# Weight loads behind all stage-one transposes, one more chunk with denominators in token order, and layer-two work chunk by chunk, in a two-layer linear-attention and MLP kernel

## The chip, the cores and the metric

One core of one Trainium2 chip. The metric is device microseconds (us) of one execution; lower is better. A kernel is compared by several timed executions, beside executions of the kernel before on the same chip. The span that a profile shows is from the first to the last instruction; in the runs here the time is the span plus about 1.75 us.

## The reference, cut to what matters

Two layers run one after the other on one sequence of 2,048 tokens with 512 features, all bf16. `A` is linear attention with 32 heads of 16, `B` an MLP of hidden size 1,792.

```python
def _A_ref(x, wqkv, wo):
    qkv = (x @ wqkv) ...                       # q, k, v: heads of 16
    phi = lambda t: jnp.where(t > 0, t + 1, jnp.exp(t)) + 1e-6
    pq, pk = phi(q), phi(k)
    kv  = jnp.einsum("bhsd,bhse->bhde", pk, v)     # a sum over ALL tokens
    z   = jnp.einsum("bhsd->bhd", pk)              # likewise
    num = jnp.einsum("bhqd,bhde->bhqe", pq, kv)
    den = jnp.einsum("bhqd,bhd->bhq", pq, z)[..., None] + 1e-6
    return (num / den) ... @ wo

def _B_ref(x, w1, b1, w2, b2):
    h = gelu(layernorm(x) @ w1 + b1)
    return h @ w2 + b2

x = A_x
for _ in range(2):                             # written out in the original
    x = x + _A_ref(_layernorm(x), A_wqkv, A_wo)
    x = x + _B_ref(_layernorm(x), B_w1, B_b1, B_w2, B_b2)
```

Because `kv` and `z` sum over all tokens, the kernel has a first stage ("stage one") that normalizes, transposes and projects all 16 tiles of 128 tokens before the first output of layer one. Four tiles are a chunk.

## The kernel before

Every operation is recorded in a graph with an engine, a duration estimate and a priority. A list scheduler then fixes the order on each engine, together with the PSUM banks and buffers. `SHIFT` moves priorities by group or name; `WAY` picks one of several ways to do the same thing (for instance, a transpose by TensorE or by DMA). The order is then replayed, each engine waiting on semaphores.

```python
def transpose(y, ykey, yT, k, key, prio, tag):          # by DMA, issued from SyncE
    ...  e.dma_start_transpose(dst, yb[:, y.slot, :])   # L647: "t<-yb" in the profile
def transpose_pe(...):                                  # by TensorE (L660), then a copy out of PSUM
    ...  e.transpose(...);  e.activation(dst(), src(), ACT.Copy)      # L670, on ACT

def attn_k(L, c, k, yT, prio):                          # K projection (L711) and phi(K)
    ...  e.matmul(bank(b), lhsT=yTa(yT)[:, dt, k*P:(k+1)*P], rhs=wqkv[:, dt, D:2*D], ...)
    phi(b, ...)                                         # exp (L681), relu (L692), min, add (L698)

def late(name, key, dst, src, prio, kb, after):         # weight loads on POOL's queue
    dma("pool", lambda e: e.dma_start(dst, src), [key], prio=prio, name=name, kb=kb, after=after)
...
pq1, trs = [], []
for c in range(NC):                                     # stage one
    for k in range(4):
        y, ykey = norm(...)
        if eng(f"TA0_{st}") == "pe":  tr = transpose_pe(...)
        else:                         tr = transpose(...)
        ...
        pk = attn_k(0, c, k, yT, pr + 3)
        attn_g_held(0, st, k, y, ykey, pk, gb, pr + 6)
    attn_z(0, c, pks, pr + cf["P_Z0"])
    trs.append(tr)                                      # the last tile of each chunk only
    attn_q(0, c, yT, pq, ...)
for h in range(2):
    late(f"w1_{h}", ..., -86 + h, 896, trs)             # L581 in the profile: four loads of 896 KB
for h in range(2):
    late(f"w2_{h}", ..., -84 + h, 896, trs)
dma("sp", lambda e: e.dma_start_transpose(b1t[:], b1r[:]), ..., name="Tb1", after=trs[-1:])
G.op("act", lambda e: e.activation(b1c[:], b1t[:, 0:FT], ACT.Copy), ..., name="b1c")
```

`Tb1` is the "bias transpose": it turns the bias of the up-projection into one column per partition, for the GELU. `b1c` is its copy on ACT. ACT works in the order that the scheduler fixed, so whatever stands behind `b1c` waits for `Tb1`.

The denominators of a chunk have two forms. By default they are four matmuls with 512 columns, then Ln and Exp on ACT. With `"den0_2": "tok"` (layer, chunk) they are a product and a reduction on POOL and DVE in token order, and a DMA transpose for each tile.

Of the kernel before, what the change touches and what calls it, by code (L numbers as in the profile page):

```python
# [19 lines left out]
NC = S // 512  # L20
# [32 lines left out]
class Op:  # L53
    __slots__ = ("eng", "fn", "dur", "lat", "deps", "tiles", "prio", "name", "table", "sem", "nbytes",
                 "idx", "start", "end", "ready", "missing", "outs", "waits", "tok", "opens", "seq", "fast", "n", "grp")

    def __init__(self, eng, fn, dur, lat, prio, name, table=None, sem=None, nbytes=0, fast=False, n=1):
        self.eng, self.fn, self.dur, self.lat = eng, fn, dur, lat
        self.prio, self.name, self.table, self.sem, self.nbytes = prio, name, table, sem, nbytes
        self.fast, self.n = fast, n  # L60
        self.deps = {}
        self.tiles = []
        self.opens = []
        self.outs = []
        self.start = self.end = None
        self.ready = 0.0
        self.tok = None
# [43 lines left out]
class Scheduler:  # L111
# [13 lines left out]
    def run(self):  # L125
        g = self.g
        for o in g.ops:
            o.missing = len(o.deps)
        for o in g.ops:
            for d in o.deps:  # L130
                d.outs.append(o)
# [11 lines left out]
        while left:  # L143
# [36 lines left out]
            at, _, o = best  # L180
            e = o.eng
# [35 lines left out]
            for w in o.outs:  # L217
                w.missing -= 1
                w.ready = max(w.ready, o.end + self.latency(o, w))
                if w.missing == 0:  # L220
                    released[w.eng].append(w)
# [70 lines left out]
def assign_waits(graph, order, sems, dma_sems):  # L292
# [10 lines left out]
    while len(done) < total:  # L303
# [45 lines left out]
    N_HALF=1, N_K=3, N_Q=2, P_Z0=7.85, N_PB=1, N_PT=8, P_DEN=-8.22, P_A2=-25.68, P_W1=-3.82, P_W2=73.83,  # L349
    P_K=47.84, P_G=106.63, P_Q=169.99, STEP=5.46, A1_Q=25.3, A1_STEP=4.8, N_H=2, N_N=2, GAP=37.5,  # L350
    TABLE_PENALTY=17.25, WINDOW=104.97,
    SHIFT={
        "B00_0": -200.0, "B00_1": -230.4, "B00_2": -43.8, "B00_3": -75.1, "B01": 573.6, "B02": 68.1,
        "B03": 1079.8, "B10_0": 139.0, "B10_1": 57.7, "B10_2": 195.5, "B10_3": 32.2, "B11": 392.5,
        "B12": 42.9, "B13": -84.8, "D00": -507.8, "D01": -19.7, "D02": 60.8, "D03": 290.1, "D0_0_3": 4.5,
        "D10": -22.9, "D11": -10.1, "D12": -16.4, "D13": 645.3, "G00_0": -7.9, "G00_1": 0.3, "G00_2": -138.2,
        "G00_3": -20.1, "G01_0": 28.9, "G01_1": -111.0, "G01_2": -39.9, "G01_3": -92.7, "G02_1": 5.5,
        "G02_2": 506.5, "G02_3": 62.7, "G03_0": -7.0, "G03_1": -43.1, "G03_2": 69.5, "G03_3": 59.5,
        "G10": 26.6, "G11": 54.3, "G12": 223.3, "G13": 8.1, "G1_2_0": 12.9, "K00_0": -436.6, "K00_1": -27.0,
        "K00_2": -31.4, "K00_3": 1.1, "K01_0": 3.7, "K01_1": -0.5, "K01_2": -12.5, "K01_3": -49.4,  # L360
        "K02_0": -2.3, "K02_1": 260.6, "K02_2": 13.8, "K03_0": 325.9, "K03_1": 272.3, "K03_2": -18.8,
        "K03_3": -116.2, "K0_0": 1.8, "K10": 76.8, "K11": 10.2, "K12": 74.9, "K13": -130.7, "K1_12": -2.7,
        "M0_2": 114.0, "N00_0": -371.7, "N00_1": -416.2, "N00_2": -206.3, "N00_3": -0.2, "N01_0": -506.7,
        "N01_1": 4.0, "N01_2": -116.3, "N01_3": 38.6, "N02_0": 7.6, "N02_1": 213.7, "N02_2": 62.3,
        "N02_3": 130.0, "N03_0": 47.7, "N03_1": 274.9, "N03_2": 165.0, "N03_3": -5.7, "N10": 29.9,
        "N11": 399.0, "N12": -2.5, "N13": 125.5, "O00_0": 113.8, "O00_1": -55.4, "O00_2": -13.0,
        "O00_3": -80.3, "O01": -191.1, "O02": 6.3, "O03": 6.1, "O10_0": 26.6, "O10_1": 179.5, "O10_2": 39.8,
        "O10_3": 196.8, "O11": -847.0, "O12": 12.5, "O13": 13.6, "OD11": -0.6, "OD8": 17.6, "PTA0_1": 5.0,
        "Q00": 486.1, "Q01": 4.9, "Q02": 544.3, "Q03": 790.2, "Q10": 264.7, "Q11": 89.7, "Q12": 850.4,
        "Q13": 202.3, "RA1_1": -1.0, "RA1_3": -2.8, "RB0_11": 5.5, "RB1_10": -4.5, "RB1_2": -2.1,  # L370
        "TA1_1": 2.6, "TA1_10": -2.5, "TA1_11": 7.6, "TA1_14": -12.7, "TB0_12": -8.0, "TB0_14": 7.8,
        "TB0_9": 5.0, "TP1_3_0": 10.2, "Tb1": 57.1, "U00_0": -32.4, "U00_1": 55.7, "U01": -34.1, "U02": -18.3,
        "U03": 10.5, "U10_1": 70.5, "U11": 17.1, "U12": -5.9, "U13": 105.3, "V0": 17.1, "V1": 34.2,
        "W00": 448.9, "W01": 288.7, "W02": -13.4, "W03": 10.3, "W10": 7.5, "W10_0_10_0": 12.9,
        "W10_0_8_0": -1.0, "W10_2_7_0": 6.9, "W10_3_9_0": 6.4, "W11": -34.5, "W11_0_6_1": -4.4,
        "W11_2_11_0": 9.4, "W12": -25.5, "W13": 58.8, "W20_3_7": -15.8, "W21_0_0": -10.8, "W21_0_7": 4.5,
        "W21_12_0": -70.7, "W21_3_7": 1.0, "W21_5_0": -0.7, "W21_5_7": 2.4, "W21_7_0": 26.0, "WO0_12_0": 34.3,
        "WO0_13_0": -36.5, "WO0_3_0": -14.3, "WO1_12_0": -21.7, "WO1_6_0": -0.7, "Z00": -23.1, "Z01": 0.8,
        "Z03": -77.1, "Z11": -19.4, "Z12": -118.0, "Z13": 27.2, "aggrB0_10": -1.5, "aggrB1_11": 10.0,
        "aggrB1_12": 4.3, "b20_8": -0.4, "b21_8": -28.4, "cpm0_1": 4.9, "cpz1": -15.6, "expk1_1": 74.7,  # L380
        "expk1_15": 5.5, "expq0_1_3": -2.2, "expq0_3_1": 2.7, "expq1_1_2": 3.4, "expq1_1_3": -1.2,
        "gelu0_0_0_1": -3.5, "gelu0_0_4_1": -26.0, "gelu0_1_2_0": -12.0, "gelu0_2_0_0": -1.8,
        "gelu0_2_6_0": -3.0, "gelu1_0_11_0": 4.6, "gelu1_0_6_0": 82.2, "gelu1_0_7_0": 1.4,
        "gelu1_0_8_1": -58.6, "gelu1_0_9_0": -48.9, "gelu1_1_5_0": 2.1, "gelu1_2_13_0": -2.6,
        "gelu1_3_6_0": -3.7, "ln0_1_0": 1.5, "ln0_2_2": -1.2, "ln0_3_3": 42.5, "mink0_1": 8.8,
        "mink0_14": -49.7, "mink1_11": -33.7, "mink1_14": -7.0, "mink1_8": 17.3, "minq0_0_0": -47.6,
        "minq0_0_3": -0.5, "minq0_3_3": -5.3, "minq1_2_3": 2.6, "nmrA0_11": 0.3, "normA0_12": 7.2,
        "normA1_0": -16.0, "normA1_10": 23.2, "normB1_3": 15.7, "phik0_10": -12.4, "phik0_15": 6.8,
        "phik0_5": 7.7, "phik0_6": -11.7, "phik0_9": 14.9, "phik1_11": 9.9, "phik1_8": 0.5,
        "phiq1_2_0": -12.4, "phiq1_3_2": -5.4, "powA0_6": -3.5, "powA1_1": -0.2, "powB0_11": 16.2,  # L390
        "powB0_3": -4.8, "pr0_0_2": -6.6, "pr0_3_0": -9.1, "pr1_0_0": 2.4, "rec0_1_3": -2.2, "rec0_2_1": -4.3,
        "rec1_0_1": -1.3, "rec1_1_3": -1.5, "reluk0_0": -5.7, "reluk0_12": 30.2, "reluk0_13": -34.0,
        "reluk0_8": -0.3, "reluk1_11": 2.2, "statsA1_12": -24.9, "statsA1_2": 3.7, "statsA1_4": 2.7,
        "statsA1_6": 8.2, "statsB0_11": 1.8, "statsB0_2": -44.8, "statsB0_3": 2.5, "statsB1_11": 3.1,
        "statsB1_4": 6.6, "tcA0_5": 10.4, "tcA0_7": 15.9, "tcB1_1": -8.8, "vepsA0_12": -2.8, "vepsA0_4": 3.8,
        "vepsA1_14": -59.9, "vepsA1_4": -3.8, "vepsB0_13": -85.9, "vepsB0_4": -1.1, "vepsB0_6": 1.3,
        "vepsB1_5": 12.9, "vepsB1_9": -27.4, "warm": -0.5, "x1": 1.4,
# [4 lines left out]
        "TA0_6": "dma", "TA0_7": "pe", "TA0_8": "pe", "TA0_9": "dma", "TA1_0": "dma", "TA1_1": "pe",  # L402
        "TA1_10": "pe", "TA1_11": "pe", "TA1_12": "pe", "TA1_13": "pe", "TA1_14": "pe", "TA1_15": "dma",
        "TA1_2": "pe", "TA1_3": "pe", "TA1_4": "pe", "TA1_5": "pe", "TA1_6": "pe", "TA1_7": "pe",
        "TA1_8": "pe", "TA1_9": "pe", "TB0_0": "dma", "TB0_1": "pe", "TB0_10": "dma", "TB0_11": "dma",
        "TB0_12": "dma", "TB0_13": "dma", "TB0_14": "dma", "TB0_15": "dma", "TB0_2": "dma", "TB0_3": "dma",
        "TB0_4": "dma", "TB0_5": "dma", "TB0_6": "dma", "TB0_7": "pe", "TB0_8": "dma", "TB0_9": "dma",
        "TB1_0": "dma", "TB1_1": "pe", "TB1_10": "dma", "TB1_11": "dma", "TB1_12": "dma", "TB1_13": "dma",
        "TB1_14": "dma", "TB1_15": "dma", "TB1_2": "dma", "TB1_3": "dma", "TB1_4": "dma", "TB1_5": "dma",
        "TB1_6": "dma", "TB1_7": "dma", "TB1_8": "dma", "TB1_9": "dma", "b20_0": "pool", "b20_1": "dve",  # L410
        "b20_10": "dve", "b20_11": "dve", "b20_12": "dve", "b20_13": "pool", "b20_14": "pool",
        "b20_15": "dve", "b20_2": "dve", "b20_3": "pool", "b20_4": "dve", "b20_5": "dve", "b20_6": "pool",
        "b20_7": "pool", "b20_8": "pool", "b20_9": "pool", "b21_0": "pool", "b21_1": "pool", "b21_10": "pool",
        "b21_11": "dve", "b21_12": "dve", "b21_13": "dve", "b21_14": "dve", "b21_15": "pool", "b21_2": "dve",
        "b21_3": "pool", "b21_4": "dve", "b21_5": "dve", "b21_6": "pool", "b21_7": "dve", "b21_8": "dve",
        "b21_9": "dve", "cpg0_0": "dve", "cpg0_1": "dve", "cpg0_2": "dve", "cpg0_3": "act", "cpg1_0": "dve",
# [39 lines left out]
def build_kernel(nc, A_x, A_wqkv, A_wo, B_x, B_w1, B_b1, B_w2, B_b2, out, conf=None, report=False):  # L456
# [5 lines left out]
    with ExitStack() as es:  # L462
# [13 lines left out]
        b1r = SB("b1r", [16, P], BF16)  # L476
# [743 lines left out]
```

## Time and profile before

| | |
|---|---|
| time, median of 3 runs | 334.19 us (334.19 to 334.74) |
| the run whose profile was kept | 336.87 us, span 335.1 us, mean granted clock 0.995 |
| first up-projection of layer one | at 70.06 us |

To the views that the prediction shows further down I add only the page's strip of 40 equal slices of 8.4 us; each digit is tenths busy, and PEclk is the granted TensorE clock in tenths:

```profile
PE   7899699999999999999999999999999999999997
PEclk9999799999999999999999999999999999999999
DMA  7814920020124003200001110001152222101001
```

In the fifth slice (33.5 to 41.9 us), PE falls to 6, the clock to 7, and the DMA engines are at 9. Nothing like it follows.

### The profile page before, as it was taken

The numbers are of one execution on the slowest core, as the hardware profiler recorded it, in microseconds if no ns is written. First come the engines' busy times: TensorE is split into PE (matmuls) and PEld (weight loads), VectorE is DVE, ScalarE is ACT, GpSimd is POOL, SyncE is SP. The second block draws the span as 40 slices with busy tenths as digits, with TensorE's granted clock in tenths as the row PEclk, the third lists the DMA queues.
The fourth block names the chain that finished last, engine by engine and source line by source line (L and its number), as shares of the span: only waits on it lengthen the run. The fifth ranks groups of instructions, "written<-read, shape, count | busy, mean of one in ns | idle before, by whom it ended". The sixth has DMA issues, their size and how long they took to land.

```text
span 335.1 us, 4774 instructions
## 1 busy us (share of the span) xinstructions
PE 326.5 (97%) x1742; PEld 160.9 (48%) x1742; DVE 214.5 (64%) x455; ACT 217.5 (65%) x366; POOL 138.1 (41%) x227
## 2 busy tenths in 40 slices
PE   7899699999999999999999999999999999999997
PEld 3444244478444444444444444447744444444444
DVE  6889466892694887205375799899899697122012
ACT  2698479999998716999623466988936601730640
POOL 5688325763483537212124362578606042020000
PEclk9999799999999999999999999999999999999999
DMA  7814920020124003200001110001152222101001
GB/s 265 268 34 85 344 92 0 2 47 2 38 56 51 16 16 80 48 0 16 18 0 31 33 32 1 2 17 33 32 120 53 63 62 66 31 6 59 16 4 60
DMA packets 40116, 18.42 MB, mean 55 GB/s; under 512 B 33756, under 2 KB 39132, under 8 KB 40092
## 3 DMA queue, kind: packets, MB, share of 16 engines
q1 hardware_dynamic: 36524, 10.90, 15.0%
q0 software_dynamic: 1056, 4.72, 4.3%
q10 hardware_dynamic: 2512, 2.49, 2.2%
q8 instruction: 14, 0.23, 0.3%
q14 instruction: 10, 0.08, 0.1%
HBM read 8.00 MB, written 2.10 MB: 30 GB/s over the span
## 4 chain that ended last, share of the span: by engine, by line
PE 86%; ACT 8%; DMA 2%; DVE 1%; issue 1%; POOL 1%
PE ps L986 29%; PE ps L1024 28%; PE ps L711 6%; PE ps L954 6%; PE ps L838 4%; PE ps L742 4%; PE ps L806 3%; DMA t<-yb 2%; PE ps L729 2%; ACT eb L681 2%; PE ps L596 1%; ACT yb L632 1%; ACT rb L692 1%; ACT lr L932 1%; PE ps L930 1%; ACT lr L934 1%
## 5 line engine op out<-in xcount | busy, mean ns | idle before, releaser
L986 PE MATMUL ps<-t,w 128*128 128x512 bf16 (+1 forms) x560 | 99.5, 336 | 0.0
L1024 PE MATMUL ps<-w,gT 128*128 128x512 bf16 x434 | 98.4, 379 | 0.0
L992 ACT ACTIVATE gT<-ps,b1c 128x512 bf16<-128x512 f32 (+1 forms) x140 | 80.5, 603 | 23.6 <-PE ps L986 23.2
L986 PEld LDWEIGHTS ps<-t,w 128*128 128x128 bf16 x560 | 54.6, 98 | 42.8 <-ACT t L670 0.6
L1024 PEld LDWEIGHTS ps<-w,gT 128*128 128x128 bf16 x434 | 42.4, 98 | 50.8
L681 ACT ACTIVATE eb<-ps 128x512 bf16<-128x512 f32 x64 | 38.6, 611 | 15.6 <-PE ps L711 13.5
L632 ACT ACTIVATE yb<-xsb,nmr,rstd 128x512 bf16<-128x512 f32 x23 | 18.5, 808 | 41.3 <-POOL nmr L629 39.0
L692 ACT ACTIVATE rb<-ps 128x512 bf16<-128x512 f32 x54 | 32.9, 616 | 12.6 <-PE ps L711 11.5
L624 POOL TENSOR_TENSOR rstd<-veps,neghalf 128x1 f32<-128x1 f32 x64 | 38.2, 597 | 6.8 <-DVE veps L622 1.9
L711 PE MATMUL ps<-wqkv,t 128*128 128x512 bf16 x128 | 32.7, 394 | 3.0 <-DMA t<-yb 2.8
L612 DVE BATCH_NORM_STATS2 stats<-xsb 128x6 f32<-128x512 f32 x48 | 32.5, 681 | 0.4
L694 DVE TENSOR_SCALAR eb<-eb 128x512 bf16<-128x512 bf16 x54 | 16.9, 319 | 23.4 <-ACT eb L681 22.9
L954 PE MATMUL ps<-gtb,t 128*128 128x512 bf16 x128 | 31.2, 379 | 0.2 <-ACT gtb L819 0.2
L938 POOL TENSOR_TENSOR t<-t,lr 128x512 bf16<-128x512 bf16 x18 | 21.6, 1199 | 18.6 <-ACT lr L934 18.6
L617 POOL TENSOR_SCALAR veps<-mv 128x1 f32<-128x1 f32 x32 | 7.0, 219 | 50.5 <-DVE mv L614 48.7
L1034 DVE TENSOR_TENSOR outb<-ps,xsb 128x512 bf16<-128x512 f32 x15 | 10.2, 682 | 26.3 <-PE ps L1024 26.2
L622 POOL TENSOR_SCALAR veps<-mv 128x1 f32<-128x1 f32 x29 | 8.1, 278 | 41.8 <-DVE mv L614 41.2
L742 PE MATMUL ps<-t,wqkv 128*128 128x512 bf16 x96 | 23.5, 379 | 0.0
L1030 DVE TENSOR_TENSOR xsb<-ps,xsb 128x512 f32<-128x512 f32 x16 | 10.9, 681 | 18.0 <-PE ps L1024 17.9
L711 PEld LDWEIGHTS ps<-wqkv,t 128*128 128x128 bf16 x128 | 12.5, 100 | 19.2 <-issue 4.9
L637 DVE TENSOR_SCALAR yb<-xsb,mv,rstd 128x512 bf16<-128x512 f32 x25 | 17.6, 703 | 4.7 <-POOL rstd L624 4.4
L959 DVE TENSOR_TENSOR xsb<-ps,xsb 128x512 f32<-128x512 f32 x16 | 10.7, 683 | 15.1 <-PE ps L954 15.1
(90 smaller groups left out, 389.2 us busy)
## 6 DMA issues: line engine op xcount, KB each, us to landing
w<-in_B_w_dram POOLq DMA_DIRECT2D x4, 896.0 KB, 9.2
out_dram<-outb SPq DMA_DIRECT2D x15, 128.0 KB, 1.8
t<-in_A_x_dram ACTq DMA_DIRECT2D x3, 512.0 KB, 8.2
t<-yb SPq DMA_TRANSPOSE x53, 2.4
wqkv<-in_A_wqkv_dram SPq DMA_DIRECT2D x1, 512.0 KB, 5.5
wqkv<-in_A_wqkv_dram ACTq DMA_DIRECT2D x1, 512.0 KB, 7.3
wqkv<-in_A_wqkv_dram POOLq DMA_DIRECT2D x1, 512.0 KB, 6.2
wo<-in_A_wo_dram POOLq DMA_DIRECT2D x1, 512.0 KB, 5.8
```

Source lines behind the costliest of these rows:

```text
L612: G.op("dve", lambda e: e.bn_stats(stats[:, s.slot, :], src()), 620, reads=src_keys, writes=[k + "s"], tiles=[s, *src_tiles], prio=prio, n ...
L624: G.op("pool", lambda e: e.tensor_tensor(rstd[:, s.slot:s.slot + 1], veps[:, s.slot:s.slot + 1], neghalf[:], op=ALU.pow), 570, reads=[k + ...
L632: G.op("act", lambda e: e.activation(yb[:, y.slot, :], src(), ACT.Identity, bias=nmr[:, s.slot:s.slot + 1], scale=rstd[:, s.slot:s.slot + 1]),
L681: G.op("act", lambda e: e.activation(eb[:, et.slot, :], bank(bt), ACT.Exp), 478, reads=[src_key], writes=[f"e{tag}"], tiles=[bt, et], prio ...
L692: G.op("act", lambda e: e.activation(rb[:, rt.slot, :], bank(bt), ACT.Relu), 478, reads=[src_key], writes=[f"r{tag}"], tiles=[bt, rt], pri ...
L711: ins = e.matmul(bank(b), lhsT=yTa(yT)[:, dt, k * P:(k + 1) * P], rhs=wqkv[:, dt, D:2 * D], start=(dt == 0), stop=(dt == DT - 1))
L742: ins = e.matmul(bank(b), lhsT=wqkv[:, dt, kt * P:(kt + 1) * P], rhs=yTa(yT)[:, dt, :], start=(dt == 0), stop=(dt == DT - 1))
L938: lambda e, kt=kt, r=r: e.tensor_tensor(yTa(pq)[:, kt, :], yTa(pq)[:, kt, :], lr[:, r.slot, :], op=ALU.mult),
L954: ins = e.matmul(bank(wb), lhsT=yTa(pq)[:, kt, k * P:(k + 1) * P], rhs=gtb[:, kt, :], start=(kt == 0), stop=(kt == DT - 1))
L986: ins = e.matmul(bank(b, n), lhsT=w1[:, dt, ft * P:(ft + 1) * P], rhs=yTa(yT)[:, dt, k0 * P:k1 * P], start=(dt == 0), stop=(dt == DT - 1))
L992: G.op("act", lambda e, ft=ft, b=b, k0=k0, k1=k1, n=n: e.activation(gT[:, g.slot, ft * 512 + k0 * P:ft * 512 + k1 * P], bank(b, n), ACT.Ge ...
L1024: ins = e.matmul(bank(b), lhsT=gT[:, g.slot, ft * 512 + k * P:ft * 512 + (k + 1) * P], rhs=w2[:, ft, :], start=(ft == 0), stop=(ft == FT - 1))
```

## The change

The intent: (1) the MLP weights shall not be loaded while stage one still needs DMA transposes, so all 16 tiles' transposes, not only the last of each chunk, go into the list that the loads wait for, and the bias transpose waits for that list too; (2) the third chunk of layer one takes its denominators in token order, which takes four matmuls from PE, adds one, and takes Ln/Exp pairs from ACT; (3) layer two's normalizations, phi(K) and G (the sum over tokens of normalized rows times phi(K)) are tied chunk to chunk by predecessors that only bind the scheduler (`soft`), so that its buffers are used in chunk order. All priorities and choices were then tuned again for the new graph.

```diff
@@ scheduler: predecessors that order, but are no data
-            o.missing = len(o.deps)
+            o.soft = [d for d in o.soft if d not in o.deps]
+            o.missing = len(o.deps) + len(o.soft)
-            for d in o.deps:
+            for d in [*o.deps, *o.soft]:
                 d.outs.append(o)
...
-                w.ready = max(w.ready, o.end + self.latency(o, w))
+                if o not in w.soft:
+                    w.ready = max(w.ready, o.end + self.latency(o, w))
@@ CONF (cut: some 200 lines of SHIFT and WAY are new throughout)
-    N_HALF=1, N_K=3, N_Q=2, P_Z0=7.85, ...  A1_Q=25.3, ...  GAP=37.5,
-    TABLE_PENALTY=17.25, WINDOW=104.97,
+    N_HALF=1, N_K=4, N_Q=2, P_Z0=0.37, ...  A1_Q=81.1, ...  GAP=0,
+    TABLE_PENALTY=25.46, WINDOW=126.58,
-        "TA0_6": "dma", "TA0_7": "pe", "TA0_8": "pe", "TA0_9": "dma", ...
+        "TA0_6": "dma", "TA0_7": "dma", "TA0_8": "dma", "TA0_9": "dma", ...
+        "den0_2": "tok", ...                      (and many phi forms)
@@ stage one
+                trs.append(tr)
                 pk = attn_k(0, c, k, yT, pr + 3)
...
             attn_z(0, c, pks, pr + cf["P_Z0"])
-            trs.append(tr)
...
-        dma("sp", ... b1t ... name="Tb1", after=trs[-1:], transpose=True)
+        dma("sp", ... b1t ... name="Tb1", after=trs, transpose=True)
@@ before the scheduler runs
+        named = {o.name: o for o in G.ops}
+        for c in range(1, NC):
+            for k in range(4):
+                for n in ("normA1_{}", "phik1_{}"):
+                    named[n.format(4 * c + k)].soft += [named[n.format(4 * (c - 1) + i)] for i in range(4)]
+                named[f"G1_{c}_{k}"].soft.append(named[f"G1_{c - 1}_{k}"])
```

Lines of the changed kernel stand six to thirteen lower in the file than before: L711 becomes L717, L986 becomes L992.

## The prediction

> **What bounds the kernel now.** I read the engine shares first, then who TensorE (PE) waited for, then the chain of work that ended last in order of time, then the stretch around the one long wait.
>
> The head of the page:
>
> ```profile
> span 335.1 us, 4774 instructions
> PE 326.5 (97%) x1742; PEld 160.9 (48%) x1742; DVE 214.5 (64%) x455; ACT 217.5 (65%) x366; POOL 138.1 (41%) x227
> ```
>
> PE is busy 97% of the span, but a busy PE need not be at its peak, so I counted its work instead. The chain gives the pitch of each kind of matmul where PE runs unhindered:
>
> ```profile
> 70.22 12.23 PE ps L986 x112
> 96.92 10.36 PE ps L986 x48
> 227.72 0.22 PE ps L660 x4
> 206.76 0.38 PE ps L787 x16
> ```
>
> That is 0.109 us for 256 columns, 0.216 us for 512, 0.055 us for a transpose or another 128-column matmul, 0.024 us for the one-column sums. Times the counts: 1,315 of 512 columns 283.8 us, 252 of 256 columns 27.5 us, 76 of 128 columns 4.1 us, 88 one-column sums 2.1 us, and the 11 warm-up matmuls 4.9 us: 322.4 us. The span is 335.1 us, so 12.7 us are lost. Cutting the chain at its own times (elapsed less work of the matmuls in that stretch) places them:
>
> - before PE's first matmul: 1.5 us
> - 1.51 to 30.52 (start of stage one): 29.0 elapsed, 26.8 work, 2.2 lost
> - 30.52 to 43.46: 12.9 elapsed, 8.15 work, **4.8 lost**
> - 43.46 to 57.31: 0.1 lost
> - 57.31 to 70.22 (to the first up-projection): 12.9 elapsed, 11.9 work, 1.0 lost
> - 70.22 to 332.66 (everything else): 262.4 elapsed, 261.8 work, 0.6 lost
> - after PE's last matmul: 2.4 us
>
> So four fifths of the run have nothing left except matmuls to remove, and one stretch holds over a third of the loss. The waits of PE, longest first, say what ended its idle time:
>
> ```profile
> PE ps L711 <- DMA t<-yb: 2.8, 1, 2.8
> PE ps L596 <- DVE onesm L560: 1.5, 1, 1.5
> PE ps L660 <- DVE yb L637: 1.0, 1, 1.0
> ```
>
> L711 is a K projection; it waited for a DMA transpose of normalized rows. The chain there:
>
> ```profile
> 29.61 0.22 DVE t L698
> 29.83 1.00 issue
> 30.82 0.16 DVE t L698
> 30.99 7.04 DMA t<-yb
> 38.03 0.14 issue
> 38.16 3.57 PE ps L711 x8
> 41.73 1.73 PE ps L742 x8
> ```
>
> That transpose was issued at 30.99 and landed 7.04 us later. Eight K matmuls after it took 3.57 us, 0.45 each, twice the usual pitch. The transposes of that stage and, in the timeline, the MLP weight loads on POOL's queue:
>
> ```profile
> DMA to landing us min/median/max: 2.4/2.5/7.0
> 30.57 1.53 POOL L581 DMA_DIRECT2D w<-in_B_w_dram  x2
> 33.20 1.90 POOL L581 DMA_DIRECT2D w<-in_B_w_dram  x2
> ```
>
> The median is 2.5 us; only the transpose issued 0.4 us after the first weight load took 7.0. The view of three windows (columns: window and its length, busy of PE, weight load, DVE, ACT, POOL, then granted clock, DMA share, GB/s) completes it:
>
> ```profile
> 26.00:31.00 5.00, 5.00 (x39) 2.53 (x38) 4.57 (x11) 5.00 (x12) 3.88 (x6) 1.00 0.35 71
> 31.00:38.10 7.10, 4.40 (x23) 1.76 (x19) 5.84 (x12) 4.00 (x8) 5.02 (x6) 1.00 0.98 262
> 38.10:43.50 5.40, 5.33 (x17) 2.09 (x18) 1.39 (x5) 2.81 (x6) 0.20 (x1) 0.68 0.98 344
> ```
>
> DMA goes from 35% to 98% busy; the granted clock falls to 0.68 after the gap. The 4.8 us are thus 2.8 us of idle PE, and about 2 us of slow matmuls after it.
>
> **What the Trainium skill says.** (1) "Perfetto Trace Analysis", section "Identifying the Most-Contended Engine": matmul busy share is no good measure of headroom. The trace agrees: 97% busy, 12.7 us lost. (2) "DMA: Bandwidth & Descriptors", section "Issuing engines are not separate DMA queues": DMAs from scalar, sync or gpsimd run on the same 16 engines and interleave. The trace agrees: a SyncE transpose beside POOL's loads took 7.0 instead of 2.5 us. (3) "TensorE: Matmul & The Clock Gate", section "HAM oscillation": idle gaps of over about 3.4 us put PE back to half clock. Here a 2.8 us gap was followed by 0.45 us matmuls, so half clock followed a gap shorter than that figure. (4) "ScalarE: Activation LUTs", section "What ACT_TABLE_LOAD costs": 1283 ns for a load plus a drain, 2.66 us together. The trace has 1,283 ns for each of 16 loads.
>
> **The change, part by part.** A list scheduler places every instruction by priorities, and the diff replaces nearly all of these; so I compared the built orders.
>
> *Weights behind all transposes.* Before, the four weight loads waited for the last tile of each chunk; a transpose issued after those fell beneath the loads. Now they wait for all of stage one's transposes (10 by DMA, 8 before). This removes the 7.0 us landing: at 2.5 us it would end at 33.5, before the K projection ahead of it ended (34.37 + 0.86 = 35.2). Saved: up to 4.8, I take 4.4 us, leaving 0.4 for ordinary unevenness. The weights come later by perhaps 3 us: their median landing was 9.2 us, so from about 34 on to 46, against a first use near 65. Hidden.
>
> *PE work.* Transposes on PE go from 44 to 40 (-4 x 0.055 = -0.22); chunk two's denominators in token order remove four denominator matmuls (-4 x 0.216 = -0.86) and add one that spreads the sums (+0.22). Q is the same count in another form. Sum -0.86 us; PE is the bound, so I count it whole.
>
> *ACT before the first GELU.* Six fewer Relu (6 x 0.62 = 3.7), two fewer Ln and Exp pairs (2 x 1.38 = 2.8), two fewer transpose copies (1.2), one fewer late normalization (0.8); three more early ones (3 x 0.84 = 2.5), one copy (0.6). Net about -5.4 us of 53 busy in the first 70. That matters: ACT stands on the chain from 53 to 68, and its work falls by more than the stall that is removed, so it should not take the stall's place.
>
> *DVE in the same stretch.* To the eighth residual add: six more max forms reading PSUM (6 x 0.69 = 4.1), three fewer normalizations (-1.5), one reduction and reciprocal (0.67 + 0.33 + 0.28), one diagonal (about 1.0), other changes near zero: +5 us on 51.7. But POOL's 2-input adds there go from 7 to 2, and DVE adds that ran beside those took up to 1.73 us instead of 0.42, so part comes back.
>
> *Later.* K may hold four PSUM banks instead of three, table loads fall from 16 to 14, and layer two's normalizations, its phi(K) and G go chunk by chunk. 0.6 us is all that these could win after 70; they can only lose.
>
> Sum: 335.1 - 4.4 - 0.86 = 329.8 us span, that is 5.3 less; from 334.19: 328.9. I add 0.5 us for new small stalls, since an order with all priorities changed is unlikely to hit the 0.6 us of the old one again: **329.4 us**.
>
> **Rivals.** *DVE becomes the bound of stage one.* For: 56 us of work in some 65. Against: the POOL adds that slowed it go. It would give back 2 to 4 us: 331.5 to 333.5. *The bias transpose stalls ACT.* It now waits for all ten transposes, and ACT's order has the bias copy before nine of its 30 exponentials; ACT could stand still for the 2.3 us that this transpose took. For: ACT runs in order. Against: four K banks absorb some. Cost 0 to 2 us: up to 331.5. *A table load or the chunk order opens a gap in the middle.* The new order puts three switch pairs among chunk two's GELUs, each pair 2.6 us of ACT beside about 3 us of PE work. Against: the old order had such pairs at 0.6 us in all. 1 to 3 us: 330.5 to 332.5. *The start gets better too.* The 2.2 and 1.0 us losses could halve with less ACT work: 327.8. *The stall is only moved:* ten transposes at 1.26 us of issue each might land late without any load beside them: 332 to 334.
>
> **Range and chances.** All removable loss gone (4.8 + 2.2 + 1.0 + 0.6, and 0.86 of work) is 9.5 us: 324.7, a floor. Over 2% faster is below 327.5, which needs 6.7 us, more than the stall and the removed work together (5.7): 0.13. Slower by 2% needs a loss larger than any above: 0.02. Range 327.2 to 332.2.
>
> **What would show it.** Right: no landing of a stage-one transpose much over 2.5 us, weight loads issued after the last of them, no PE wait of over 1 us on a DMA, a clock near 1.00 in every window after the warm-up, first up-projection near 65 instead of 70.2. PE's count lower by four transposes and three 512-column matmuls. Wrong: a new PE wait on DVE or ACT between 20 and 65, ACT idle before the bias copy, or the time from the first up-projection to the last matmul over 263 us, which was 262.4.

## The result, and the profile after

The changed kernel takes 334.14 us (median of 4 runs, 333.71 to 334.76), against 334.19 us (334.11 to 334.74, 4 runs) for the kernel before. The ratio is 0.9996, with a 95% interval of 0.9976 to 1.0017: the same. A ratio here is the mean time of one kernel's runs over the mean of the other's runs of the same rounds, so not quite the ratio of the medians. Executions over 1.5% slower than the fastest of the same kernel are left out of the means. The prediction was 329.4 us with a range of 327.2 to 332.2; the measured time lies outside it.

The head of the page after:

```profile
span 332.2 us, 4772 instructions
PE 324.7 (98%) x1735; PEld 159.6 (48%) x1735; DVE 219.1 (66%) x461; ACT 208.7 (63%) x348; POOL 146.8 (44%) x238
```

The span fell by 2.9 us against the profile before, while the time did not fall. The two profiles are thus not of runs that stand for their kernels in the same way; the first experiment settles that. PE's waits after, longest first (in all us, how often, longest):

```profile
PE ps L602 <- DVE onesm L566: 1.5, 1, 1.5
PE ps L793 <- DVE pkb L704: 0.8, 1, 0.8
PE ps L717 <- DMA t<-yb: 0.7, 2, 0.4
PE ps L666 <- DVE yb L643: 0.6, 1, 0.6
PE ps L992 <- ACT t L676: 0.4, 1, 0.4
```

The 2.8 us wait for a transpose is gone. No single wait of size has come in its place, but several small ones have. The first new one is L793, the one-column sums over phi(K). In the chain in order of time (start, us, what), what releases it is the bias transpose:

```profile
31.50 2.39 DMA t<-yb
...
33.91 4.61 DMA b1t<-b1r
...
38.55 0.21 ACT b1c L1085
38.76 0.48 ACT eb L687
39.24 0.50 ACT rb L698
...
39.83 0.44 DVE pkb L704
...
40.31 0.55 PE ps L793 x16
```

The last stage-one transpose lands at 33.89. That releases both the bias transpose, at 33.91, and the weight loads, of which the trace shows the first at 34.2 and the last at 36.7. The bias transpose takes 4.61 us to land; in the profile before it took 2.3. The next line is ACT's wait, from ACT's view of 8 to 70 us:

```profile
ACT b1c L1085 <- DMA b1t<-b1r: 1.4, 1, 1.4
```

ACT stands still for 1.4 us, then exp, relu and the addition follow one after another, and PE loses 0.8 us. The landings of stage one's ten transposes, in one line:

```profile
DMA to landing us min/median/max: 2.4/2.5/4.2
```

None takes 7.0 us any more. But one takes 4.2 and two more over 3 us, with no weight load beside them. So the prediction's last rival ("the stall is only moved") came true in part; what these landings share is shown after the last run of the changed kernel.

To place the loss I took each kernel's trace, counted its matmuls at the unhindered pitch as the prediction does, and cut at the first up-projection of layer one and of layer two. All in us:

| profile of | span | clock | work | lost in stage one | in layer one | in layer two and tail |
|---|---|---|---|---|---|---|
| before, the one kept | 335.1 | 0.995 | 322.4 | 9.48 | 0.54 | 2.69 |
| before, again | 332.8 | 1.000 | 322.4 | 7.17 | 0.56 | 2.68 |
| changed | 332.2 | 1.000 | 321.5 | 6.13 | 1.84 | 2.71 |
| changed, again | 333.0 | 1.000 | 321.5 | 6.97 | 1.86 | 2.70 |

So the changed kernel saves its 0.86 us of work, saves only 0.2 to 1.0 us in stage one against a run of before at full clock, and loses 1.3 us more in layer one.

### The profile page after: what moved, and what is told of

Read it like the earlier page. It is cut to its first block, busy times and chain, and to the rows that moved or that the text cites. A ratio compares the mean times of both kernels' runs of the same rounds, so it can differ in the third digit from the quotient of the medians.

```text
span 332.2 us, 4772 instructions
## 1 busy us (share of the span) xinstructions
PE 324.7 (98%) x1735; PEld 159.6 (48%) x1735; DVE 219.1 (66%) x461; ACT 208.7 (63%) x348; POOL 146.8 (44%) x238
## 4 chain that ended last, share of the span: by engine, by line
PE 78%; DVE 9%; DMA 5%; POOL 4%; ACT 3%; issue 1%; DVEq 0%; POOLq 0%
PE ps L1030 27%; PE ps L992 26%; PE ps L960 8%; PE ps L717 4%; PE ps L748 3%; PE ps L844 3%; DMA t<-yb 3%; PE ps L735 2%; PE ps L812 2%; POOL rstd L630 2%; DMA b1t<-b1r 1%; DVE gtb L828 1%; DVE yb L643 1%; DVE stats L618 1%; DMA t<-in_A_x_dram 1%; PE ps L936 1%
## 5 line engine op out<-in xcount | busy, mean ns | idle before, releaser
L992 PE MATMUL ps<-t,w 128*128 128x512 bf16 (+1 forms) x560 | 99.3, 337 | 0.4 <-ACT t L676 0.4
L1030 PE MATMUL ps<-w,gT 128*128 128x512 bf16 x434 | 97.3, 379 | 0.0
L992 PEld LDWEIGHTS ps<-t,w 128*128 128x128 bf16 x560 | 54.5, 98 | 44.0 <-ACT t L676 1.5
L717 PE MATMUL ps<-wqkv,t 128*128 128x512 bf16 x128 | 30.9, 380 | 1.2 <-DMA t<-yb 0.7
L944 POOL TENSOR_TENSOR t<-t,lr 128x512 bf16<-128x512 bf16 x10 | 11.6, 1163 | 36.4 <-ACT lr L940 36.4
L623 POOL TENSOR_SCALAR veps<-mv 128x1 f32<-128x1 f32 x32 | 8.8, 274 | 41.2 <-DVE mv L620 39.5
L698 ACT ACTIVATE rb<-ps 128x512 bf16<-128x512 f32 x41 | 24.8, 609 | 3.3 <-PE ps L748 2.3
L1036 DVE TENSOR_TENSOR xsb<-ps,xsb 128x512 f32<-128x512 f32 x16 | 10.7, 675 | 23.7 <-PE ps L1030 23.7
L977 POOL TENSOR_TENSOR xsb<-xsb,b2b 128x512 f32<-128x512 f32 x19 | 22.5, 1192 | 3.1 <-DVE yb L643 2.0
L700 DVE TENSOR_SCALAR eb<-eb 128x512 bf16<-128x512 bf16 x41 | 15.1, 378 | 11.2 <-ACT eb L687 11.1
L628 POOL TENSOR_SCALAR veps<-mv 128x1 f32<-128x1 f32 x29 | 7.4, 257 | 32.8 <-DVE mv L620 31.5
L717 PEld LDWEIGHTS ps<-wqkv,t 128*128 128x128 bf16 x128 | 11.9, 97 | 16.2 <-ACT t L676 0.9
L748 PE MATMUL ps<-t,wqkv 128*128 128x512 bf16 x80 | 19.6, 379 | 0.0
L960 PEld LDWEIGHTS ps<-gtb,t 128*128 128x128 bf16 x128 | 12.3, 98 | 15.2 <-DVE gtb L828 1.2
```

Source lines behind the costliest of these rows:

```text
L698: G.op("act", lambda e: e.activation(rb[:, rt.slot, :], bank(bt), ACT.Relu), 478, reads=[src_key], writes=[f"r{tag}"], tiles=[bt, rt], pri ...
L717: ins = e.matmul(bank(b), lhsT=yTa(yT)[:, dt, k * P:(k + 1) * P], rhs=wqkv[:, dt, D:2 * D], start=(dt == 0), stop=(dt == DT - 1))
L748: ins = e.matmul(bank(b), lhsT=wqkv[:, dt, kt * P:(kt + 1) * P], rhs=yTa(yT)[:, dt, :], start=(dt == 0), stop=(dt == DT - 1))
L960: ins = e.matmul(bank(wb), lhsT=yTa(pq)[:, kt, k * P:(k + 1) * P], rhs=gtb[:, kt, :], start=(kt == 0), stop=(kt == DT - 1))
L977: G.op("pool" if on_pool else "dve", lambda e: e.tensor_tensor(xsb[:, st, :], xsb[:, st, :], b2b[:], op=ALU.add), 1120 if on_pool else 600 ...
L992: ins = e.matmul(bank(b, n), lhsT=w1[:, dt, ft * P:(ft + 1) * P], rhs=yTa(yT)[:, dt, k0 * P:k1 * P], start=(dt == 0), stop=(dt == DT - 1))
```

## The experiments

There were thirteen runs of ten kernels; all gave correct results. They ran on different chips, so each is compared through the runs of before on its own chip. "Lower group" and "upper group" are explained with the first of them.

**b_again: the kernel before, unchanged.** The question is whether the profile kept was of an ordinary run.

> The kernel before, unchanged, to see its runs one by one. In the profile on record of before, the run took 336.87 us with a span of 335.1 us and a clock of 0.995, while its timed runs had a median of 334.19 us. Theory A (the profiled run was not typical: the half clock after the gap is paid in some runs only): most runs have a span near 332.5 us and a clock of 1.00, and a profile in which the transpose still lands after some 7 us and PE still waits 2 to 3 us, but the eight K matmuls after it take 1.7 us, not 3.6. Theory B (the profile was typical, and something else lengthens it against the timed runs): spans near 335 us and clocks of 0.995 throughout. Time 334.2 us in both.

Measured: 334.26, 334.37, 334.57, 334.79, and 335.73, 336.04 us; the runs of before beside it lay at 334.15 to 334.94 (four) and 336.12 to 336.83 (seven), with nothing between. Every run of the lower group had a granted clock of 0.999 or 1.0, every run of the upper one 0.995. Over all experiments 21 of 50 executions of before were in the upper group, which by chip was 1.5 to 2.0 us slower in the mean. (Both groups count in the ratios quoted here, so a ratio also depends on how many upper runs of before a chip had. The differences of means against the lower group do not.) The profile kept was one of these (336.87), while the median to be beaten, 334.19, was of the lower group. The new profile is of the lower group. Its chain and its longest wait:

```profile
30.54 6.75 DMA t<-yb
37.29 0.14 issue
37.42 1.89 PE ps L711 x8
```

```profile
PE ps L711 <- DMA t<-yb: 2.6, 1, 2.6
```

The transpose is as late as before (6.75 against 7.04 us), and PE idles as long. But the eight K matmuls take 1.89 us instead of 3.57: no low clock follows. What follows from it: the "about 2 us of slow matmuls" of the prediction were not in the time that was to be lowered. Only the gap of 2.6 us was.

**b_filler: before, with PE kept busy in the gap.** Twelve spare matmuls run ahead of the K projection that waits for the late transpose. Their result is overwritten.

```diff
+                if o.name == "K0_13":          # after its other waits, ahead of its wait for the transpose
+                    for _ in range(12):
+                        e.matmul(bank(bt), lhsT=onesm[:, 0:P], rhs=onesm[:, :], start=True, stop=True)
```

> The kernel before, with 12 spare matmuls of 512 columns (12 x 0.216 = 2.6 us, into the PSUM bank that the waiting K projection overwrites) put into the gap in which PE waits for the late transpose; nothing else is moved, and the transpose still lands after about 7 us. The runs of before fall into two groups, near 334.4 and near 336.5 us. Theory A (the upper group pays for matmuls at half clock after this gap): with PE kept busy the upper group disappears and all runs lie near 334.4 us. Rival (the two groups have another cause, the start of the kernel or the memory): about half of the runs stay near 336.5 us.

Measured: 334.63 us (334.27 to 335.21), ratio 0.9991 (0.9963 to 1.0019). All six runs had a clock of 1.0, against three of eleven of before beside it with 0.995 (335.98 to 336.67). The chain shows the spare matmuls in the gap's place:

```profile
34.77 0.86 PE ps L713 x4
35.63 2.59 PE ps L1168 x12
38.22 1.73 PE ps L713 x8
```

The gap is as long as ever, but filled, and the upper group does not appear. So, as far as six runs can say, the low clock of the upper group comes from the idle gap, and it and the gap are two separate costs: filling the gap removes the first alone. (Six runs without an upper one are not many. At 21 of 50 the chance of that is (29/50)^6, about 4%; at this chip's own 3 of 11 it is (8/11)^6, about 15%. The twelve runs of b_behind_bias and best_again, in which the gap is gone, are all at full clock as well. Other kernels show that a low clock is not tied to this gap alone: see b_behind and bb_tok.)

**b_behind: before, with the weight loads behind all transposes, alone.** The order on PE, ACT, DVE and SyncE does not change; on POOL one addition changes places with its neighbour. The bias transpose keeps its old place.

```diff
+                trs.append(tr)
                 pk = attn_k(0, c, k, yT, pr + 3)
...
-            trs.append(tr)
...
-        ... name="Tb1", after=trs[-1:], ...
+        ... name="Tb1", after=trs[15:], ...
```

> The kernel before with one part of the change alone: the weight loads wait for every transpose of stage one (the bias transpose keeps its place; the order on PE, ACT, DVE and SP is the same, on POOL one phi add passes the loads). Theory A: the 7.0 us landing becomes 2.5 us, PE's wait for it goes, and the time falls by the gap alone, 2 to 2.8 us, to 331.4 to 332.2 us. Theory B: the whole 4.8 us come back, 329.4 us. Theory C (ACT or DVE is the bound of stage one anyway): under 1 us, 333.2 us or more.

Measured: 332.18 us (331.82 to 332.58 but for the profiled run, 334.44, whose clock was 0.69 between 10 and 15 us, near its start, after PE had waited for DVE three times, 1.1 us at the longest); ratio 0.9904 (0.987 to 0.9938). The mean of its five undisturbed runs, 332.15, lies 2.3 us below the mean of before's lower group on that chip, 334.46. The first part of the change works, and alone it is worth what the gap was worth.

**b_behind_bias and best_again: the same, with the bias transpose behind all transposes too,** so the whole first part of the change on the old priorities. It was run twice, on two chips.

```diff
-        ... name="Tb1", after=trs[-1:], ...
+        ... name="Tb1", after=trs, ...
```

> The kernel before with the whole first part of the change: weight loads and the bias transpose behind all transposes of stage one. Theory D (the bias transpose, issued together with the weight loads, inherits part of the stall): it lands after 4 to 5 us, ACT stands before the bias copy, and the time is 0.8 to 2 us above that of the run with the weights alone behind the transposes (332.2 us), so 333.0 to 334.2 us. Rival (hidden): within 0.4 us of 332.2 us.

> The kernel before with only the first part of the change (weights and bias behind all transposes), a second time, beside the repaired versions of the changed kernel on one chip. Expected 332.3 us and no run above 333 us; so 2.0 us below the lower group of before and below the changed kernel, and 0.5 to 1.5 us below the repaired versions, because these still carry about 0.8 us more loss in layer one and more in stage one, against 0.86 us less work on PE.

Measured: 332.35 us (332.05 to 332.54), ratio 0.992 (0.9893 to 0.9947); and 332.19 us (331.85 to 332.61), ratio 0.9917 (0.9892 to 0.9942). Twelve runs, all at a clock of 0.999 or 1.0. PE's chain has no gap where it was (profile of b_behind_bias):

```profile
31.80 0.86 PE ps L711 x4
32.66 1.73 PE ps L742 x8
34.39 2.59 PE ps L711 x12
```

Stage one loses 4.98 and 4.53 us in the two profiles, instead of 7.17. In this order the bias transpose landed in 2.3 us and ACT did not wait for it, so what its new place costs depends on the order around it. The traces show one difference. Here the bias transpose was issued 0.6 to 0.7 us before the first weight load (at 32.09 against 32.80, and at 31.72 against 32.35); in the changed kernel it was 0.27 us (33.91 against 34.18). Over all profiles, of the transposes in flight beside the weight loads, those issued at least 0.6 us before the first load landed within 2.8 us, those 0.27 us before it after 4.56 to 4.61, one at the same moment (0.01 us before it) after 5.88, and those 0.40 to 0.55 us after it after 6.45 to 7.04. No run varies this lead alone. This is the fastest kernel; it beats both the kernel before and the changed one by about 2 us.

**a_unbehind: the changed kernel, with the weight loads behind the last tile of each chunk again.** This undoes the first part alone.

```diff
-                trs.append(tr)
+                trs.append(tr) if k == 3 else None
...
-        ... name="Tb1", after=trs, ...
+        ... name="Tb1", after=trs[-1:], ...
```

> The changed kernel with the weight loads again behind the last tile of each chunk only, and the bias transpose early. If the collision is what matters (A and B), the loads start while some of the ten transposes are still to come, landings of 4 to 10 us appear, and the time rises by 2 to 5 us, to 336 to 339 us. Theory C: no change within 1 us.

Measured: 335.12 us; four runs at 333.65 to 335.14 and two slow (342.66 and 343.28); ratio of the fast runs 0.9961 (0.9923 to 0.9999). One transpose took 5.9 us to land in its profile, but PE waited only 1.1 us there (the view puts that wait down to DVE, which finished within 0.01 us of the landing). The expected 336 to 339 us did not come. In the new order undoing the first part costs little: its four fast runs have a mean of 334.44, the changed kernel's runs elsewhere 334.19 to 334.71. The run also moves the bias transpose early, so it undoes two things at once; the next run separates them.

**a_b1early: the changed kernel, with only the bias transpose released earlier** (after the last tile's transpose, as in the order of a_unbehind, weights still behind all ten).

```diff
-        ... name="Tb1", after=trs, ...
+        ... name="Tb1", after=trs[15:], ...
```

> The changed kernel with the bias transpose early again, weights still behind all ten transposes; the order of all engines is that of the run before this one. In the profile after, the bias transpose is issued with the weight loads, lands after 4.6 us, and ACT stands 1.4 us before the bias copy, PE 0.8 us behind it. Theory D (the stall was handed to the bias transpose and costs time): 0.8 to 1.5 us faster than the changed kernel, 332.6 to 333.3 us. Rival (this wait is hidden by PE's queue of work): under 0.4 us, 333.8 to 334.2 us.

Measured: 333.22 us (332.55 to 334.63), ratio 0.9929 (0.9897 to 0.9962), about 1.1 us below before's lower group on that chip (333.38 against 334.46, means). Its profiled run was its slowest; there PE waited 1.8 us for one DMA transpose, which landed after 4.6 us with no weight load in flight. By the means, the loads' place in the new order is worth about 1 us (334.44 of a_unbehind against 333.38), but with four and six runs that spread over 1.5 and 2.1 us the 95% interval of this difference is about -0.2 to 2.3 us, so it is not clear of noise. The bias transpose's place looks worth about as much, against runs of the changed kernel on other chips. This release also changes the order on ACT, DVE and SyncE a little, so I then moved the transpose by itself.

**a_b1first: the changed kernel, with the bias transpose ahead of stage one's ten other transposes.** All else keeps its order.

```diff
         order = sch.run()
+        tb = by["Tb1"]
+        for t in trs:
+            tb.deps.pop(t, None)
+        order["sp"].remove(tb)
+        order["sp"].insert(1 + max(i for i, o in enumerate(order["sp"]) if o.name in ("b1", "b2")), tb)
```

> The changed kernel with one thing moved: the bias transpose goes ahead of the ten stage-one transposes on SyncE's queue, as soon as the bias row has landed; every other order stays, and the weights stay behind the ten transposes. In two profiles of the changed kernel the bias copy on ACT waited 1.3 to 1.4 us and PE 0.7 to 0.8 us behind it. Theory D (this wait costs time): the wait goes, and the time is 0.7 to 1.4 us below 334.4 us, 333.0 to 333.7 us, loss of stage one about 5.5 us. Rival (hidden by the next wait): 334.0 us or more.

Measured: 333.27 us (332.81 to 334.18), ratio 0.9955 (0.9925 to 0.9985). ACT no longer waits for the bias, PE's wait at L793 is gone, and stage one loses 5.11 us instead of 6.13. But the changed kernel had not run on this chip, and the intervals overlap. Hence the next three.

**a_again, a_again2 and a_b1first2: the changed kernel unchanged, twice; the second time beside a_b1first on one chip.**

> The changed kernel, unchanged, beside before on this chip, since the chip of the second set showed before mostly in its upper group. Theory A: the changed kernel has no gap over 1 us in stage one, so it stays near 334.1 us with no upper group, while before has both; its advantage is then 0 us against the lower group and about 2.2 us against the upper. Rival: it has an upper group too.

> The changed kernel once more, unchanged, only to stand on one chip and in one batch beside the kernel with its bias transpose first. Both theories: ratio to before between 0.997 and 1.003, about 334.3 us if before is at 334.3.

> The changed kernel with only the bias transpose moved ahead of stage one's other transposes, as once before, now beside the changed kernel on the same chip. Theory: issuing the bias transpose together with the weight loads costs 0.8 to 1.4 us, so this comes out 0.8 to 1.4 us below the changed kernel of this batch (ratio to before near 0.996). Rival: the earlier difference was between chips and batches, and here the two agree within 0.4 us.

Measured: a_again 334.7 us (333.85 to 335.05, and one of 336.22 with a clock of 0.997), ratio 0.9995 (0.9963 to 1.0026). Then, on one chip: a_again2 334.82 us (333.86 to 335.08), ratio 0.999 (0.9966 to 1.0014), and a_b1first2 333.8 us (332.66 to 334.39), ratio 0.9955 (0.9931 to 0.9979). The means of the six runs are 334.71 and 333.72: the bias transpose in its new place costs 1.0 us (95% interval about 0.3 to 1.7). The profiles agree: the first up-projection came at 66.06 and 66.01 us in after and a_again2, at 65.04 and 65.08 in a_b1first and a_b1first2. In a_again2's profile the line of the chain

```profile
33.91 4.56 DMA b1t<-b1r
```

stands again where it stood in the first profile after, with a wait of 1.0 us at L793; in a_b1first2 there is no wait at L793. Of 16 executions of the changed kernel, one was in an upper group, against 21 of 50 of before. So in the mean over all these executions the changed kernel comes out 0.6 us better (334.62 against 335.25), though that mixes chips; the ratios quoted here do not show it.

**a_fix2: a_b1first, and a copy moved ahead of a table load.** In layer one the changed kernel loses 1.3 us more than before. The chain of the changed kernel shows one place:

```profile
82.90 1.28 ACT L1169
...
84.20 0.60 ACT eb L687
84.79 0.50 ACT t L676
...
85.34 1.90 PE ps L992 x8
```

L1169 is the load of the exp table. The copy L676 completes the transposed input of chunk two's up-projection (L992). It stands behind the table load and an exp, and PE waits 0.4 us for it; the first matmuls after it are not at pitch either (1.90 us instead of 1.73 for eight).

```diff
+        # in addition to the edit of a_b1first:
+        act = order["act"]
+        i = ...                      # that copy; act[i - 1] is the exp ahead of it
+        act[i - 1], act[i] = act[i], act[i - 1]
```

The table load is placed by the replay in front of the first exp, so this swap moves the copy ahead of both.

> The run before this one, and also the copy of a transposed tile moved ahead of the table load and exponential that stand before it on ACT, just before chunk two's up-projection; PE waited 0.4 us for that copy in two profiles. If that wait is one of the losses that the new order brought to layer one: 0.4 to 0.6 us below the run before, and loss of layer one 1.3 instead of 1.84 us. Rival: the load is only pushed before the GELUs, which then wait, and nothing is won.

Measured: 333.26 us (332.25 to 333.66, and one of 335.75 with a clock of 0.995), ratio 0.9953 (0.9917 to 0.9988). In the profile the loss of layer one fell from 1.86 to 1.25 us, and the stop at 85 us is gone, so that place is found. The time hardly fell (means 332.94 against 333.39 for a_b1first on that chip, within the spread of either): in its profile, stage one had a wait of 1.6 us for a DMA transpose that a_b1first's did not have.

**What the late transposes share.** The view of the DMA queues for 25.8 to 30.0 us of the profile after, in which the transpose of 4.2 us was in flight, names a queue besides that of the transposes:

```profile
q8 instruction: 1, 0.02, 2.2%
```

This is one packet of 16 KB. I went through the transposes issued between 16 and 60 us in all fifteen profiles. With neither a weight load nor a packet of an "instruction" queue in flight, all 81 landed within 2.6 us. With such a packet and no load, 23 of 53 took 2.95 to 4.62 us, all 23 in the new order; and no late landing without a load lacks one. No run moves these packets, so this is a coincidence that always held, not a cause shown.

**bb_tok: b_behind, with token order for the third chunk, on the old priorities.**

```diff
-        ... "den1_2": "tok",
+        ... "den0_2": "tok", "den1_2": "tok",
```

> The kernel before with the weights behind all transposes, and chunk two's denominators of layer one in token order as the second part of the change (priorities otherwise those of before). Three matmuls of 0.216 us fewer on PE. If PE's count is all that it changes: 0.6 us below 332.2 us, 331.6 us. If the order that the scheduler finds with the old priorities opens new gaps, as I fear of the change itself: 332.5 to 335 us.

Measured: 338.87 us (338.26 to 339.89, clocks of 0.99 to 0.995), ratio 1.0112 (1.0081 to 1.0142), so 6.7 us slower than b_behind (338.87 - 332.18). The scheduler finds another order nearly everywhere. PE's longest wait is now an up-projection waiting for ACT, that is for a GELU of earlier banks:

```profile
PE ps L986 <- ACT gT L992: 3.2, 2, 2.9
```

The loss is in layer two (9.2 us instead of 2.7). Some 3 us of it are a low clock, by an estimate: after this wait of 2.9 us, PE's clock in the profile is 0.54 from 230.0 to 237.5 us (0.46 x 7.5 = 3.45 us, less the start of that stretch, in which PE still waited). The loss lies where token order for a chunk of layer one has no operation at all. So the run says nothing about the cost of token order. It says how much the list scheduler's order reacts to a single choice.

**What could not be tried.** The changed kernel without the `soft` rules, without `den0_2` in token order, with its two added DMA transposes back on TensorE, or with the bias transpose released after the first tile: none of the four can be built, because the scheduler comes to a point at which no operation can start. A fourth K bank (`N_K=4`) alone on the kernel before builds, but changes no engine's order, so it was not run.

## Why the prediction was wrong

**The mechanism of the first part: right.** A transpose fell beneath the weight loads and took 7.0 us; with the loads behind all transposes, it does not. The weight loads came late without harm, as predicted. Doing this alone gained 2.0 to 2.3 us.

**The size, "Saved: up to 4.8, I take 4.4 us": wrong, and the first failed step.** The 4.8 us were the sum of 2.8 us of idle PE and about 2 us of slow matmuls, read from one profile. That profile was of a run of 336.87 us, 2.7 us above the median of 334.19 that I then subtracted from. The slow matmuls belonged to the upper group alone: b_again shows the same gap without them, and b_filler shows them gone when the gap is filled. The profiled run's own time stood beside the median from the start. Comparing the two would have said that part of the stall was not in the median. The term should have been about 2.2 us: the idle gap alone.

**PE work, -0.86 us: right as a count.** The matmuls went from 1,742 to 1,735, the work from 322.4 to 321.5 us. No run isolates what this is worth in time.

**ACT, -5.4 us before the first GELU: nearly right in size.** ACT was busy 52.8 us to the first up-projection before and 47.9 after. What that bought is not isolated. But the conclusion drawn from it, that ACT "should not take the stall's place", failed: ACT stood still for the bias for 1.4 us. **DVE, +5 us: too high.** It was busy 53.4 us to the first up-projection, against 51.4 to 51.7 before, and was not the bound of stage one.

**"I add 0.5 us for new small stalls": wrong, and the second failed step.** The stalls measured:

- The bias transpose behind all transposes: 1.0 us. It is now released at the same moment as the weight loads (0.27 us before the first of them), lands after 4.6 instead of 2.3 us, and stalls ACT. The prediction named this as its second rival, with 0 to 2 us, and counted nothing for it. It took the landing to be 2.3 us as before, though its own argument, that transposes beside weight loads land late, applies to this one as well.
- Layer one: 1.3 us (1.84 against 0.55). The prediction named this as a rival too, with 1 to 3 us. Of it, 0.6 us is the copy behind the table load, by the profiles. The other 0.7 us is several waits of 0.2 to 0.4 us in the trace; no run isolates these.
- Small waits for DMA transposes in stage one that differ from run to run (0 to 1.8 us in the profiles of the new order). With the terms above, the sum from before's lower group is -2.2 - 0.86 + 1.0 + 1.3 = -0.8 us, or about 333.6 from its means near 334.4. The changed kernel's means lie at 334.2 to 334.7, so some 0.6 to 1.1 us are left over. That these waits are the remainder is argued from single profiles, not shown.

**The signs that the prediction had set.** All three of its signs of being wrong came: a new wait of PE on DVE between 20 and 65 us (0.8 us at L793), ACT idle before the bias copy (1.4 us), and 263.6 us from the first up-projection to the last matmul, where it had named 263. Of its signs of being right, the landings (up to 4.2 us) and the first up-projection (at 66.06 us, not near 65) missed.

**What stays open:** whether the "instruction" packets delay the transposes of the changed order or only come with the delay; what token order and the `soft` rules do by themselves; and why the same gap lowers the clock in some executions and not in others. The gaps of the two profiles, 2.8 us (low clock) and 2.6 us (not), lie too close together to tell a threshold from chance. The wait of 2.9 us in bb_tok was followed by a low clock, but so were waits of at most 1.1 us in b_behind.

The experiments point to the first part of the change on the old priorities as the better kernel: 332.2 to 332.35 us, 0.8% below before by the ratios of both of its runs, and 0.6 to 0.7% below its lower group.

## What to carry to other kernels

Before pricing a stall from a profile, compare the time of the profiled run with the median: what only the slower runs pay cannot be gained from the median. When transfers are put behind a set of events to stop a collision, look for everything else released by the same event, because it now collides instead. And when a good local change comes together with a new order for everything, run the local change on the old order as well; here that was the better kernel.

## What the Trainium skill lacked or had wrong

- "TensorE: Matmul & The Clock Gate", section "HAM oscillation": idle gaps above about 3.4 us are named as what lowers the clock. Here a gap of 2.8 us was followed by eight matmuls in 3.57 us instead of 1.73 in one profile, and one of 2.6 us by eight in 1.89 us in another. 21 of 50 executions of before had a clock of 0.995 and took 1.5 to 2.0 us longer; with the gap filled by spare matmuls, none of six. So gaps below that figure can cost a low clock, in some executions only.
- "DMA: Bandwidth & Descriptors", section "Rules for kernel authors": a transpose next to ordinary DMAs "needs nothing". That is said of correctness, and the results were correct; the page gives no duration for the case. Here a 128x512 transpose issued just after the first weight load landed after 6.45 to 7.04 us and after 2.5 us without (medians of stage one), and the bias transpose after 4.6 instead of 2.3. Nor does any page that I found say that transposes land late beside a packet of an "instruction" queue, as 23 of them did here (2.95 to 4.62 us).
- "ScalarE: Activation LUTs", section "What ACT_TABLE_LOAD costs": 1283 ns for the load and a drain of about 1380 ns besides. The load agrees (1.28 us), but in the chain of the changed kernel the exp starts at 84.20, 0.02 us after the load that began at 82.90 ends, and the load began 0.02 us after the instruction before it: no such drain is visible here.
- "TensorE: Matmul & The Clock Gate", section "What's actually happening", says that the same kernel varies from run to run in how many slow matmuls it has at its start. No page that I found says the same of a gap in the middle: here one kernel with one fixed order had two groups of run times 1.5 to 2.0 us apart, by the clock after one gap.
